# Sliding-window attention and a gated MLP on one Trainium2 core: all loads issued by GpSimd and cast to f16 on the way

## The chip, the cores and the metric

The kernel runs on one core of one Trainium2 chip. A core has five engines with an instruction stream each: TensorE (PE, matmuls into PSUM), VectorE (DVE), ScalarE (ACT), GpSimd (POOL) and SyncE (SP). Sixteen DMA engines move data between HBM and the on-chip memory SBUF; a DMA is issued from an engine's queue. The metric is the device time of one launch in microseconds (us), as the median of several runs.

## The reference

Eight batches, eight heads, 576 positions, head size 64, everything in float32. Attention over a causal window of 64 positions, then a gated MLP that mixes along the sequence:

```python
scores = (q @ k.T) / sqrt(64)                      # per batch and head
mask   = (rel >= 0) & (rel < 64)                   # rel = query position - key position
attn   = softmax(where(mask, scores, -1e9))
x      = (attn @ v) as [batch, 576, 8 * 64]
h      = relu(x @ w_in)                            # 512 -> 1024
u, v   = h[..., :512], h[..., 512:]
v_n    = (v - mean(v)) / sqrt(var(v) + 1e-6)       # over the 512 features
v_s    = w_spatial @ v_n + b_spatial               # along the sequence, 576 x 576
out    = (u * v_s) @ w_out                         # 512 -> 512
```

## The kernel before, in words

The work is cut into named steps, and a list in the source, `ORDER`, gives for every step its engine and its buffer or PSUM bank. `as_listed` takes the steps in the order of that list, so the list alone sets the order in which each engine meets its work; every engine runs its own steps strictly in that order and waits where a result or a buffer is not there yet. The planner's costs that stand at each step (such as `("DQ", 0.45)`) are not read when the kernel is built.

A step's name tells what it is. `b` is the batch (0 to 7), `g` the half of the heads (0, 1), `u` a pair of heads' sets within the half, `j` and `i` blocks of 128 positions or features.

- `ldk`, `ldq`, `ldv`: loads of k, q and v; `ldwin`, `ldwsp`, `ldb`, `ldwo`: loads of the weights. All are issued by SP (written DQ in the list), in float32, into staging tiles (`nat`, eight buffers, and `natv`, four).
- `ck`, `cq`, `cv`, `cwin`, `cwsp`, `cb`, `cwo`: casts from the staging tile to f16, on DVE, ACT or POOL, as the list says. They all go through the helper `cp` (L292 for ACT, L295, L298 and L300 for the others; the POOL forms are cut into pieces).
- `tk`, `tq`: transposes of k and q on DVE, in blocks of 32 x 32 pairs (L419). `sl`, `su`, `s4`: copies of v that shift it by 64 rows, from `hv` into `hs`.
- `S`: scores on PE (L479); `E`: exp on ACT (L486); `M`: the mask, a minimum with a constant tile on DVE (L489); `Z`: column sums (L502); `N`, `n`: the inverse of the sums, as exp(-ln) on ACT; `P`: the product with v (L514); `X`: the scaling, on DVE (L522). `_r` marks the last 64 positions, done apart.
- `V`: the half of the first MLP matmul that is normalised; `Vr` (relu, ACT), `Vb`, `Va` (mean and variance, DVE), `L1`, `L2` (ACT), `A` (the normalisation, DVE, L728). `U`, `Ur`: the other half. `W`, `We`: transposes of w_spatial. `G`: the spatial matmul; `Ge`: the gate on DVE (L797, L800). `O`: the output matmul; `Oe`: its copy out of PSUM; `st`: the store, issued by SP and at the end by ACT as well. `V4` of a batch carries the last block of `O` of the batch before.
- `D0` to `D26`: matmuls on a tile of zeros (L862), which keep PE busy while it waits at the start.

PE steps marked `PH` are issued as two matmuls of 64 columns of weights each (`halves`, L617), the others as one (L614). The constants come first, outside the list: the mask tile is built from `keep` by seven DVE instructions (L252 to L258), the identity and two rows of ones by POOL. The buffers matter as well: `hqk` (q and k in f16) has four, `hv` and `hs` (v and its shifted copy) four each.

Of the kernel before, what the change touches and what calls it, by code (L numbers as in the profile page):

```python
# [18 lines left out]
D24:PE:0 ldb:DQ:0 D5:PE:1 D21:PE:2 ldk0_0:DQ:1 ck0_0:DVE:0 tk0_0:DVE:0 D18:PE:3 D2:PE:2 D14:PE:2  # L19
D19:PE:3 D10:PE:0 ldq0_0:DQ:2 ldk0_1:DQ:3 ldv0_00:DQ:0 ldq0_1:DQ:4 ldv0_10:DQ:1 D3:PE:3 ldv0_11:DQ  # L20
cv0_10:POOL:0 ldk1_0:DQ:5 ck0_1:ACT:1 ldv0_12:DQ ldv0_13:DQ ldv0_01:DQ cq0_0:DVE:2 ldq1_0:DQ:6
tq0_0:DVE:1 ldv0_02:DQ D1:PE:2 S0_0:PE:0:1 tk0_1:DVE:2 D22:PE:0 E0_01:ACT:0 E0_00:ACT:1 cq0_1:DVE:3
tq0_1:DVE:3 D15:PE:3 D6:PE:1 D0:PE:2 D26:PE:0 D23:PE:3 S0_r:PE:1:0 E0_r0:ACT:0 E0_r1:ACT cv0_11:POOL
sl0_10:DVE:0 M0_00:DVE ldv0_03:DQ su0_10:DVE M0_01:DVE ck1_0:DVE:0 M0_r:DVE D8:PE:1 Z0_00:PE:2
ldv0_04:DQ ldwin110:DQ:7 ldv0_14:DQ ldwin111:DQ ldwin100:DQ:1 S0_1:PE:1:0 N0_00:ACT:0 E0_11:ACT:2
D16:PE:0 D7:PE:3 E0_10:ACT:3 M0_11:DVE Z0_01:PE:1 Z0_r:PE:2 D4:PE:0 Z0_11:PE:3 N0_r:ACT:1
N0_01:ACT:2 cv0_00:ACT:1 N0_11:ACT:3 ldwin101:DQ su0_11:DVE M0_10:DVE D12:PE:0 Z0_10:PE:2 D20:PE:1
sl0_11:POOL tk1_0:DVE:4 sl0_00:ACT:1 N0_10:ACT:4 n0_11:ACT n0_10:ACT cq1_0:POOL:2 tq1_0:DVE:5
ldq1_1:DQ:2 ldk1_1:DQ:3 P0_10:PE:0 P0_11:PE:3 cwin110:ACT n0_01:ACT D11:PE:1 cv0_01:POOL
ldwin000:DQ:4 ldwin010:DQ:5 ldwin001:DQ ldwin011:DQ ldwsp1:DQ:6 X0_10:DVE:0 su0_00:DVE X0_11:DVE  # L30
n0_00:ACT sl0_01:POOL cb:POOL su0_01:POOL S1_0:PE:0:1 D25:PE:2 D13:PE:1 P0_00:PE:0 X0_00:DVE:1
E1_01:ACT:3 s40_1:ACT P0_01:PE:2 D9:PE:3 cwin111:POOL cwin100:POOL cwin101:POOL ck1_1:POOL:1
s40_0:ACT E1_00:ACT:2 cwin010:POOL X0_01:DVE cwin001:POOL cwin011:POOL V0_2:PE:1 M1_01:DVE
Vr0_2:ACT:0 n0_r:ACT P0_r:PE:3 Z1_01:PE:0 V0_0:PE:2 ldwsp3:DQ:0 M1_00:DVE N1_01:ACT:5 Vr0_0:ACT:1
cq1_1:DVE:3 Z1_00:PE:1 V0_3:PH:0 V0_1:PE:2 N1_00:ACT:4 cwin000:ACT Vr0_3:ACT:2 Vr0_1:ACT:3
ldwsp0:DQ:7 ldwsp4:DQ:1 ldwsp2:DQ:2 cwsp1:POOL:6 ldv1_00:DQ:2 ldq2_0:DQ:3 X0_r:DVE:0 tq1_1:DVE:7
Vb0_2:DVE:0 V0_4:PE:3 tk1_1:DVE:8 S1_1:PE:1:0 cwsp3:POOL:0 cwsp0:POOL:1 Vb0_0:DVE:1 Vb0_3:DVE:2
Vr0_4:ACT:4 Va0_3:DVE Vb0_4:DVE:3 Va0_4:DVE Va0_0:DVE Va0_2:DVE Vb0_1:DVE:4 Va0_1:DVE U0_2:PH:1
U0_3:PH:0 ldk2_0:DQ:4 U0_4:PE:2 ldv1_01:DQ ldv1_02:DQ ldv1_03:DQ E1_11:ACT:1 E1_10:ACT:0 cwsp2:POOL
cq2_0:POOL:0 M1_10:DVE ldv1_10:DQ:3 Ur0_2:ACT:0 L10:ACT:0 ldv1_11:DQ ldv1_12:DQ ldv1_13:DQ L20:ACT  # L40
ldv1_14:DQ ldq2_1:DQ:5 ldv1_04:DQ ldk2_1:DQ:6 ldwo00:DQ:0 ldwo01:DQ Ur0_4:ACT:1 S1_r:PE:0:1
Z1_10:PE:3 U0_0:PE:1 ldwo10:DQ:7 ldwo11:DQ U0_1:PE:2 E1_r0:ACT:0 Ur0_3:ACT:2 E1_r1:ACT Ur0_0:ACT:3
N1_10:ACT:3 A0_0:DVE:0 A0_3:DVE:1 cwsp4:DVE Ur0_1:ACT:4 W1:PE:0 W3:PE:1 W2:PE:3 W0:PE:2 A0_1:DVE:2
A0_4:DVE M1_11:DVE We1:DVE M1_r:DVE n1_00:ACT We2:ACT We3:ACT A0_2:DVE:3 We0:DVE W4:PE:0 ldq3_0:DQ:1
ldk3_0:DQ:2 ldv2_00:DQ:1 ck2_0:POOL:2 We4:DVE D17:PE:3 Z1_11:PE:1 Z1_r:PE:2 G0_0:PH:3 G0_1:PH:0
tq2_0:DVE:2 n1_10:ACT N1_11:ACT:0 tk2_0:DVE:3 Ge0_0:DVE:0 cv1_00:ACT:2 n1_01:ACT sl1_00:POOL:2
n1_11:ACT su1_00:ACT N1_r:ACT:2 cv1_01:POOL Ge0_1:DVE:1 su1_01:DVE G0_3:PH:1 sl1_01:POOL
cv1_10:ACT:3 Ge0_3:DVE:2 cv1_11:DVE S2_0:PE:0:1 P1_01:PE:2 P1_00:PE:3 X1_00:DVE:2 G0_2:PH:0
sl1_10:POOL:3 ldv2_01:DQ ldv2_02:DQ su1_10:ACT sl1_11:ACT E2_01:ACT:3 n1_r:ACT su1_11:POOL
s41_1:POOL P1_10:PE:1 X1_01:DVE P1_11:PE:3 G0_4:PE:2 X1_10:DVE:3 X1_11:DVE U1_1:PH:1 cq2_1:POOL:3  # L50
E2_00:ACT:2 M2_01:DVE Ur1_1:ACT:5 Ge0_4:DVE:3 ck2_1:POOL:1 ldv2_03:DQ V1_2:PH:3 cwo01:POOL
cwo10:POOL cwo11:POOL Ge0_2:DVE:4 M2_00:DVE Z2_01:PE:2 s41_0:ACT Vr1_2:ACT:5 N2_01:ACT:1 U1_2:PH:1
Ur1_2:ACT:3 P1_r:PE:0 V1_1:PH:3 Vr1_1:ACT:6 cq3_0:POOL:0 Z2_00:PE:2 V1_3:PE:1 tq2_1:DVE:4
# [147 lines left out]
def kernel(  # L201
# [100 lines left out]
    def cost(n, a=True, d=True, p=True, d1=False):  # L302
# [613 lines left out]
```

## Time and profile before

| | us |
|---|---|
| median of 3 runs | 195.66 (195.64 to 197.04) |
| span of the profiled execution, from the first to the last instruction | 193.6 |
| PE busy | 184.9 |
| DVE busy | 163.7 |
| ACT busy | 157.1 |
| POOL busy | 87.4 |

The page gives no time of its own for the profiled execution beside the span; the median of the runs lies 2.1 us above that span. The granted TensorE clock is 1.00 in every stretch of the profile. Busy time does not count instructions that issue DMAs. Lines such as L489 are lines of the kernel before.

### The profile page before, as it was taken

To read this page: it belongs to the slowest core of one execution; us is meant where nothing else is said; L and a number is where in the kernel's file an instruction comes from. 1 tells how busy PE (TensorE), PEld (TensorE's weight loads), DVE (VectorE), ACT (ScalarE), POOL (GpSimd) and SP (SyncE) were. 2 spreads that over 40 slices of the span, in tenths; PEclk is the share of its full clock that TensorE was granted. 3 is DMA by queue.
4 is the path that set the end of the run, shared out by engine and by line. 5 is a ranking of instruction groups with operands and counts; after the bars stand their busy time and mean duration, and the time that the engine had idled before them with its cause. 6 is when DMAs were issued, how large, how long until landed. Compare 5 with 4: busy or idle time off the path is not lost.

```text
span 193.6 us, 7606 instructions
## 1 busy us (share of the span) xinstructions
PE 184.9 (95%) x3218; PEld 107.0 (55%) x3218; DVE 163.7 (85%) x304; ACT 157.1 (81%) x282; POOL 87.4 (45%) x161
## 2 busy tenths in 40 slices
PE   7798998999999999999999999999999999999991
PEld 2352534556556664656665656565756565665560
DVE  4899899999999999998999999998996967468331
ACT  2269998998999999899979999999999875706430
POOL 4027775849932986701956577615641520000000
PEclk9999999999999999999999999999999999999999
DMA  5999999899989997619987999669958000600445
GB/s 177 373 316 290 391 355 333 168 275 373 242 205 332 261 335 179 149 38 289 367 230 184 310 310 282 196 177 218 306 125 266 22 3 0 224 30 0 135 166 191
DMA packets 50421, 42.73 MB, mean 221 GB/s; under 512 B 39377, under 2 KB 39761, under 8 KB 50386
## 3 DMA queue, kind: packets, MB, share of 16 engines
q1 hardware_dynamic: 50162, 42.04, 73.3%
q8 instruction: 25, 0.41, 0.9%
q10 hardware_dynamic: 224, 0.20, 0.3%
q14 instruction: 10, 0.08, 0.1%
HBM read 32.79 MB, written 9.44 MB: 218 GB/s over the span
## 4 chain that ended last, share of the span: by engine, by line
PE 70%; DVE 13%; ACT 9%; DMA 3%; issue 2%; SPq 1%
PE bank L617 50%; PE bank L614 4%; PE pair L479 4%; PE bank L514 3%; DMA nk<-in_k_dram 3%; PE bank L502 3%; ACT e L486 3%; DVE qT L419 2%; PE bank L702 2%; DVE e L489 2%; DVE kT L419 2%; DVE st L671 2%; DVE g L797 1%; DVE x L522 1%; ACT lz L529 1%
## 5 line engine op out<-in xcount | busy, mean ns | idle before, releaser
L617 PE MATMUL bank<-wspT,vn 128*64 128x512 f16 (+3 forms) x530 | 39.1, 296 | 0.0
L486 ACT ACTIVATE e<-pair 128x1024 f16<-128x1024 f32 x32 | 32.0, 1030 | 1.6 <-PE pair L479 1.4
L797 DVE TENSOR_TENSOR g<-bank,ru 128x512 f16<-128x512 f32 (+1 forms) x36 | 23.3, 654 | 9.4 <-PE bank L617 7.0
L647 ACT COPY ob<-bank 128x512 f32<-128x512 f32 (+1 forms) x38 | 21.9, 591 | 9.7 <-PE bank L617 8.4
L669 ACT ACTIVATE vs<-bank 128x512 f16<-128x512 f32 (+1 forms) x40 | 23.8, 602 | 7.1 <-PE bank L705 5.6
L617 PE MATMUL bank<-x,win 128*64 128x512 f16 (+2 forms) x304 | 29.1, 327 | 0.0
L617 PEld LDWEIGHTS <-vn 128*64 128x64 f16 (+1 forms) x530 | 20.8, 111 | 13.2 <-issue 0.2
L671 DVE BATCH_NORM_STATS2 st<-vs 128x6 f32<-128x512 f16 (+1 forms) x40 | 26.0, 670 | 2.3 <-ACT vs L669 2.2
L298 POOL COPY hs<-hv 64x512 f16<-64x512 f16 (+1 forms) x36 | 20.1, 585 | 16.3 <-ACT hv L292 8.4
L617 PE MATMUL bank<-win,x 128*64 128x512 f16 x216 | 27.0, 379 | 0.0
L617 PE MATMUL bank<-wout,g 128*64 128x512 f16 (+1 forms) x208 | 24.7, 371 | 0.0
L522 DVE TENSOR_TENSOR x<-bank,lz 128x512 f16<-128x512 f32 x32 | 21.2, 684 | 3.5 <-PE bank L514 2.2
L489 DVE TENSOR_TENSOR e<-e,mask 128x1024 f16<-128x1024 f16 x32 | 23.0, 725 | 0.5 <-ACT e L486 0.4
L763 ACT ACTIVATE ru<-bank 128x512 f32<-128x512 f32 (+1 forms) x38 | 21.6, 584 | 1.5 <-PE bank L617 0.8
L295 POOL CAST hk<-nk 128x384 f16<-128x384 f32 x36 | 19.4, 574 | 7.1 <-DMA nk<-in_k_dram 6.7
L529 ACT ACTIVATE lz<-bank 128x512 f32<-128x512 f32 x32 | 19.0, 599 | 1.9 <-PE bank L502 1.6
L298 POOL CAST hv<-nv 128x512 f16<-128x512 f32 x18 | 11.7, 661 | 18.8 <-DMA nv<-in_v_dram 18.7
L419 DVE STREAM_TRANSPOSE kT<-hk 128x576 f32<-128x576 f32 x16 | 19.9, 1241 | 0.2 <-ACT hk L292 0.2
L419 DVE STREAM_TRANSPOSE qT<-hq 128x576 f32<-128x576 f32 x16 | 19.8, 1237 | 0.2
L531 ACT ACTIVATE lz<-lz 128x512 f32<-128x512 f32 x32 | 19.6, 642 | 0.0
L295 POOL CAST hq<-nq 128x384 f16<-128x384 f32 x27 | 14.9, 588 | 10.3 <-DMA nq<-in_q_dram 7.8
L617 PEld LDWEIGHTS <-win 128*64 128x64 f16 x304 | 14.4, 110 | 9.2
(91 smaller groups left out, 298.9 us busy)
## 6 DMA issues: line engine op xcount, KB each, us to landing
nk<-in_k_dram SPq DMA_DIRECT2D x16, 576.0 KB, 6.6
nq<-in_q_dram SPq DMA_DIRECT2D x16, 576.0 KB, 6.1
nv<-in_v_dram SPq DMA_DIRECT2D x64, 128.0 KB, 5.9
out_dram<-ob SPq DMA_DIRECT2D x14, 512.0 KB, 5.8
wi<-in_moe_w_in_dram SPq DMA_DIRECT2D x8, 256.0 KB, 5.8
ws<-in_moe_w_spatial_dram SPq DMA_DIRECT2D x4, 288.0 KB, 7.6
nv<-in_v_dram SPq DMA_DIRECT2D x16, 64.0 KB, 4.5
wo<-in_moe_w_out_dram SPq DMA_DIRECT2D x4, 256.0 KB, 7.2
```

The lines of the kernel that those rows point to most:

```text
L295: nc.gpsimd.tensor_copy(o[:, n:n + 384], i[:, n:n + 384])
L298: nc.gpsimd.tensor_copy(o[:, lo:hi, :, :], i[:, lo:hi, :, :])
L419: d = add(f"t{name}{b}_{g}", ("DVE", 1.09), key, lambda e: nc.vector.transpose(qt.t[:, :].rearrange("p (i j) -> p j i", j=18), h.t[:, :].b ...
L486: ex = add(f"E{b}_{g}{u}", ("ACT", 0.91), key, lambda e, u=u: nc.scalar.activation(e2[u].t[:, :, :], sc[u].t[:, :, :], AF.Exp, bias=0.0, s ...
L489: mins.append(add(f"M{b}_{g}{u}", ("DVE", 0.65), key, lambda e, u=u: nc.vector.tensor_tensor(e2[u].t[:, :, :], e2[u].t[:, :, :], mask[:, : ...
L522: lambda e, u=u, ob=ob, lz=lz: nc.vector.tensor_tensor(x.t[:, u, :], ob.t[:, :], lz.t[:, :], ALU.mult),
L617: nc.tensor.matmul(o[c:c + 64, :], w[:, c:c + 64], x, start=start, stop=stop)
L647: lambda e: (nc.vector.tensor_copy if last else nc.scalar.copy)(view(), m.t[rows, 0:n]),
L669: rl = add(f"Vr{b}_{j}", ("ACT", 0.49), key, lambda e: nc.scalar.activation(vs.t[0:jn, :], m.t[0:jn, :], AF.Relu), deps=[pv], acq=[vs], us ...
L671: s1 = add(f"Vb{b}_{j}", ("DVE", 0.6), key + 0.02, lambda e: nc.vector.bn_stats(st6.t[0:jn, 0:6], vs.t[0:jn, :]), deps=[rl], acq=[st6], us ...
L763: lambda e, m=m, ru=ru, n=n: nc.scalar.activation(ru.t[:, 0:n], m.t[:, 0:n], AF.Relu), deps=[pu], acq=[ru], uses=[m])))
L797: nc.vector.tensor_tensor(g.t[:, 0:n], m.t[:, 0:n], ru.t[:, 0:n], ALU.mult)
```

## The change

No load is issued by SP any more. Each load is issued by POOL, from the float32 tensor in HBM into a f16 tile, so the DMA casts it on the way; v too goes straight into `hv`. The staging tiles and all casts of loads on chip are gone. The weights come in few DMAs (two for w_in, two for w_spatial, one for w_out), into merged tiles. `hqk` and `hv` have eight buffers instead of four. The mask and the constants become steps of the list: `keep` and `consts` on POOL, `mask` on DVE, and the mask minimum waits for `mask`. 38 warm-up steps stand in the place of 27 (13 of two matmuls, 25 of one, all over 512 columns), and the whole list is in a new order, with new engines for the shifted copies of v, and other PSUM banks.

The core of the diff (of the list only the first lines of the new one and its part around the end of the attention):

```diff
 ORDER = """
...
+D0:PE:0 D1:PE:1 D2:PE:2 D3:PE:3 D4:PE:0 D5:PE:1 D6:PE:2 D7:PE:3 D8:PE:0 D9:PE:1 D10:PE:2 D11:PE:3
+D12:PE:0 ldq0_0:POOL:0 ldk0_0:POOL:1 tk0_0:DVE:0 ldq0_1:POOL:2 tq0_0:DVE:1 S0_0:PE:0:1 tq0_1:DVE:2
+E0_00:ACT:0 E0_01:ACT:1 ldk0_1:POOL:3 tk0_1:DVE:3 keep:POOL mask:DVE M0_00:DVE M0_01:DVE D13:PE:1
...
+N6_11:ACT:1 n6_11:ACT E7_10:ACT:1 E7_11:ACT:0 sl7_00:POOL:3 su7_00:POOL ldv7_10:POOL:6 Va5_1:DVE
+X6_10:DVE:1 X6_11:DVE M7_00:DVE O4_0:PH:1 U5_1:PH:2 M7_10:DVE Va5_0:DVE O4_1:PH:3 Oe4_0:ACT:1
+Ur5_1:ACT:3 Vb5_2:DVE:3 V6_3:PH:0 Vr6_3:ACT:5 Va5_2:DVE M7_11:DVE S7_r:PE:0:1 Vb6_3:DVE:2
+Z7_11:PE:1 N7_11:ACT:4 s47_0:DVE Va5_4:DVE Z7_10:PE:2 N7_10:ACT:3 L15:ACT:1 L25:ACT Oe4_1:ACT
+A5_1:DVE:4 A5_4:DVE O4_2:PH:0 Oe4_2:ACT:0 V6_0:PH:1 sl7_10:POOL:2 ldv7_14:POOL Vr6_0:ACT:6
+s47_1:POOL s46_1:POOL U5_0:PH:2 Ur5_0:ACT:5 V6_1:PH:3 Z7_00:PE:0 O4_3:PH:1 N7_00:ACT:5 Oe4_3:ACT
...
-NWARM, NFILL, FILL = 27, 2, 9
-BUFS = {"nat": 8, "natv": 4, "hqk": 4, "qkT": 9, "hv": 4, "hs": 4, "e2": 4, "er": 1, "lz": 6,
+NWARM, NFILL, FILL = 38, 25, 1
+BUFS = {"hqk": 8, "qkT": 9, "hv": 8, "hs": 4, "e2": 4, "er": 1, "lz": 6,
...
+    kept = add("keep", ("POOL", 0.7), -2.0, emit_keep)
+    masked = add("mask", ("DVE", 2.0), -2.0, emit_mask, deps=[kept])
+    def emit_consts(e):
+        make_identity(nc, id16[:])
+        for i in range(NSB):
+            nc.gpsimd.memset(vn4_t[i][64:65, :], 1.0)
+    ids = add("consts", ("POOL", 1.8), -2.0, emit_consts)
...
+            ld = add(f"ldwin{half}", ("POOL", 0.85), key + 0.01 * (1 - half),
+                     lambda e, cs=cs: nc.gpsimd.dma_start(
+                         w_in_all[:, :, cs], moe_w_in[:, cs].rearrange("(r p) f -> p r f", r=4)))
...
+            add("ldwsp0", ("POOL", 0.85), key, lambda e: nc.gpsimd.dma_start(
+                wsp_nat[:, 0:4, :], moe_w_spatial[0:512, :].rearrange("(t p) s -> p t s", t=4))),
...
-            n = buf("nat", f"n{name}{b}_{g}")
-            ld = add(f"ld{name}{b}_{g}", ("DQ", 0.45), key, lambda e: nc.sync.dma_start(
-                n.t[:, :], src[b, 4 * g:4 * g + 4, :, :].rearrange("h (i j) d -> (h i) (j d)", j=18)),
-                acq=[n], nbytes=1.57, n=128)
             h = buf("hqk", f"h{name}{b}_{g}")
-            c = add(f"c{name}{b}_{g}", cost(1152), key,
-                    lambda e: cp(e, h.t[:, :], n.t[:, :]), deps=[ld], acq=[h], uses=[n])
+            ld = add(f"ld{name}{b}_{g}", ("POOL", 0.55), key, lambda e: nc.gpsimd.dma_start(
+                h.t[:, :], src[b, 4 * g:4 * g + 4, :, :].rearrange("h (i j) d -> (h i) (j d)", j=18)),
+                acq=[h])
...
+            ld = add(f"ldv{b}_{g}{n}", ("POOL", 0.5 + 0.36 * w), key + 0.002 + 0.0001 * n,
+                     lambda e, lo=lo, hi=hi: [nc.gpsimd.dma_start(
+                         hv.t[:, c, :, :],
+                         v[b, 4 * g:4 * g + 4, 128 * c:128 * c + 128, :].transpose([1, 0, 2]))
+                         for c in range(lo, hi)],
+                     deps=done[:1], acq=[hv] if n == 0 else [], uses=[hv] if n else [])
...
+        ld = add(f"ldv{b}_{g}4", ("POOL", 0.65), key + 0.0025, lambda e: nc.gpsimd.dma_start(
+            hv.t[0:64, 4, :, :], v[b, 4 * g:4 * g + 4, 512:576, :].transpose([1, 0, 2])),
+            deps=[done[0]], uses=[hv])
...
-                n = 512 if i < NWARM - NFILL else 128
+                n = 512
```

More of the change, by code (lines that the diff above doesn't have):

```diff
@@ L24 @@
[L24 to L53, printed above, removed]
@@ L120 @@
-E7_00:ACT:3 Oe4_4:ACT:0 X6_11:DVE Vr5_4:ACT:4 cq7_1:ACT:1 O4_0:PH:0 Oe4_0:ACT:0 M7_00:DVE Va5_0:DVE
-M7_01:DVE Vb5_4:DVE:1 U6_2:PH:2 O4_1:PH:1 V6_0:PH:3 O4_2:PH:0 Ur6_2:ACT:5 Oe4_1:ACT st4_0:DQ
-Vr6_0:ACT:2 cv7_00:POOL:2 Va5_2:DVE tk7_1:DVE:5 Va5_4:DVE tq7_1:DVE:6 L15:ACT:1 L25:ACT A5_0:DVE:4
-A5_2:DVE:5 Oe4_2:ACT:1 Z7_01:PE:2 Z7_00:PE:1 O4_3:PH:3 N7_01:ACT:1 N7_00:ACT:5 Oe4_3:ACT V6_1:PH:0
-S7_1:PE:1:0 V6_3:PH:2 sl7_00:POOL:2 A5_1:DVE:6 A5_4:DVE A5_3:DVE:7 G5_3:PH:1 Vr6_1:ACT:0 Vb6_1:DVE:0
-su7_00:POOL ldv7_13:DQ E7_11:ACT:0 E7_10:ACT:2 n7_00:ACT P7_00:PE:3 G5_4:PH:0 S7_r:PE:0:1
@@ L292, in cp @@
             nc.scalar.copy(o, i)
-        elif e == "POOL" and len(i.shape) == 2 and i.shape[1] > 1000:
-            for n in (0, 384, 768):
-                nc.gpsimd.tensor_copy(o[:, n:n + 384], i[:, n:n + 384])
         elif e == "POOL" and len(i.shape) == 4 and i.shape[1] > 2:
```

332 lines of the change are left out of this document (143 added, 189 removed).

## The prediction

> **What bounds the kernel now.** I read the page first: the shares, the slices, and the chain that ended last.
>
> ```profile
> PE 184.9 (95%) x3218; PEld 107.0 (55%) x3218; DVE 163.7 (85%) x304; ACT 157.1 (81%) x282; POOL 87.4 (45%) x161
> ...
> GB/s 177 373 316 290 391 355 333 168 275 373 242 205 332 261 335 179 149 38 289 367 230 184 310 310 282 196 177 218 306 125 266 22 3 0 224 30 0 135 166 191
> ...
> PE 70%; DVE 13%; ACT 9%; DMA 3%; issue 2%; SPq 1%
> ```
>
> TensorE (PE) is busy in 95% of the span and carries 70% of the chain, so only what shortens PE's own list, its start or its tail can help. The busy time is not all work. The warm-up matmuls have a group of their own, 16.1 us, in the grouped lines; then I cut the span into stretches (columns: length, then PE, PEld, DVE, ACT, POOL busy, granted clock, DMA share, GB/s).
>
> ```profile
> L862 PE MATMUL bank<-scratch 128*128 128x512 f16 (+1 forms) x68 | 16.1, 380 | 1.3 <-DVE scratch L237 1.3
> ```
>
> ```profile
> 5.26:38.69 33.43, 30.46 (x493) 14.98 (x492) 31.66 (x52) 26.90 (x48) 19.46 (x29) 1.00 1.05 317
> 38.69:60.00 21.31, 21.26 (x432) 12.00 (x428) 20.51 (x37) 20.02 (x38) 12.80 (x23) 1.00 0.93 284
> 60.00:100.00 40.00, 39.67 (x706) 24.82 (x697) 38.64 (x71) 37.82 (x70) 23.57 (x44) 1.00 0.84 242
> 100.00:140.00 40.00, 40.00 (x884) 24.60 (x874) 37.45 (x64) 38.44 (x67) 22.79 (x43) 1.00 0.87 240
> 140.00:152.07 12.07, 12.07 (x248) 7.17 (x246) 10.29 (x22) 11.95 (x21) 2.73 (x5) 1.00 0.63 175
> 152.07:189.45 37.38, 37.38 (x490) 21.94 (x486) 22.82 (x51) 20.31 (x40) 3.72 (x6) 1.00 0.23 78
> ```
>
> From 38.69 us on, PE is packed; ahead of it lies the filler. But VectorE (DVE) is nearly as full: 31.66 of 33.43 us in the first stretch, 97% from 60 to 100. So two engines are critical at once: DVE sets the start, PE the rest, and DVE follows it closely until the last attention steps.
>
> **The point at which I compare.** Z7_11, the column sums of the last batch's last pair of heads, is where DVE's heavy work ends. It starts at 152.07 us. Up to there DVE has been busy for 31.66+20.51+38.64+37.45+10.29 = 138.6 of 146.8 us since 5.26, so it was idle for 8.2. Behind it PE has 37.4 us left.
>
> ```profile
> 152.07 0.38 PE L502 MATMUL bank<-e,ones 128*64 128x512 f16 x2
> ...
> 177.04 3.62 PE L617 MATMUL bank<-wout,g 128*64 128x512 f16 x32
> 180.50 5.14 PE L617 MATMUL bank<-wspT,vn 128*64 128x512 f16 x80
> 185.46 3.20 PE L617 MATMUL bank<-wout,g 128*64 128x512 f16 x32
> ...
> 190.31 0.54 ACTq L838 DMA_DIRECT2D out_dram<-ob  x1
> ```
>
> The last row is the last store, issued second on ACT's queue; from the end of PE (189.45) to the end of the span (193.6) it is 4.15 us. Starts of neighbours give PE's prices: four O steps in 180.50-177.04 = 3.46, so 0.865 each, or 0.216 for 512 columns (V and U are as long); five G steps in 185.46-180.50 = 4.96.
>
> **The new list, PE.** Counting the two lists: behind Z7_11 the new one has all the steps that the old one has there, and 13 more: O4_2, O4_3, U5_0, U6_2, V6_0, V6_1 (6 x 0.865 = 5.2), G5_2 to G5_4 (3.0) and four short Z and P steps (each passes 512 columns through both halves of the array side by side: 0.22, so 0.9). So PE has 37.4+9.1 = 46.5 us left. The work is the same; attention has moved 9 us earlier against the rest. DVE must therefore be done with it about 9 us earlier, and 8.2 us of idle time is what it had.
>
> **The new list, DVE, up to that point.** Rows for what is removed, added and moved:
>
> ```profile
> L300 DVE CAST hq<-nq 128x1152 f16<-128x1152 f32 x4 | 3.3, 826 | 0.0
> L300 DVE CAST hk<-nk 128x1152 f16<-128x1152 f32 x2 | 1.9, 965 | 1.7 <-DMA nk<-in_k_dram 1.7
> L300 DVE COPY hs<-hv 64x512 f16<-64x512 f16 x4 | 1.2, 294 | 0.1
> L300 DVE COPY hs<-hv 64x768 f16<-64x768 f16 x1 | 0.7, 655 | 0.0
> L300 DVE COPY hs<-hv 64x1024 f16<-64x1024 f16 x1 | 0.4, 422 | 0.0
> L300 DVE COPY hs<-hv 64x256 f16<-64x256 f16 x1 | 0.2, 222 | 0.0
> ...
> L728 DVE TENSOR_SCALAR vn<-vs,mv,ln 128x512 f16<-128x512 f16 x32 | 12.1, 422 | 2.2 <-ACT ln L718 1.9
> L522 DVE TENSOR_TENSOR x<-bank,lz 128x512 f16<-128x512 f32 x32 | 21.2, 684 | 3.5 <-PE bank L514 2.2
> ```
>
> ```profile
> 0.81 0.15 POOL L244 MEMSET keep<- 128x64 f16 x1 [0.29 <-POOLq L902]
> 1.21 0.38 SPq L412 DMA_DIRECT2D nk<-in_k_dram  x1
> 1.61 0.18 DVE L252 COPY mask<-keep 128x64 f16<-128x64 f16 x1 [0.32 <-POOL keep L247]
> 3.27 0.29 DVE L258 COPY mask<-mask 128x512 f16<-128x512 f16 x1
> 5.26 0.76 DVE L300 CAST hk<-nk 128x1152 f16<-128x1152 f32 x1 [1.66 <-DMA nk<-in_k_dram]
> 8.20 1.15 ACT L292 CAST hk<-nk 128x1152 f16<-128x1152 f32 x1 [6.11 <-DMA nk<-in_k_dram]
> 38.69 3.42 PE L617 MATMUL bank<-wspT,vn 128*64 128x512 f16 x30
> ```
>
> Removed: six q/k casts, 5.2 us, and three smaller casts, about 1.4 at the price of the 64x1024 copy and above; 6.2 in all after an overlap of 0.06 each with the neighbour (my estimate: the groups add up to some 16 us more than the 163.7 busy, over 304 instructions). Moved: the seven mask steps ran from 1.61 to 3.56 while DVE waited for its first load; in the new list they stand after four transposes, on the path: +1.95. Copies into hs: eight before; 25 now, of which 15 are small (0.22 to 0.29), one kind is 64x1024 (0.42, 3) and one 64x768 (6, between 0.35, the larger copy's price scaled, and the 0.655 of its single row); with the overlap +3.5 to +5.3. I take +3.5, because the larger copy needed only 0.42. The order leaves for later five A steps (0.42), one X and, at its price, one Vb and one Ge (0.68 each) and small ones: -4.2. Sum: 138.6-6.2+1.95+3.5-4.2 = 133.7.
>
> **Contention.** The mask minimum (M) is one form throughout, and yet:
>
> ```profile
> L489 DVE TENSOR_TENSOR e<-e,mask x32: 649/682/1062, 12.8 to 151.8; 128x1024 f16<-128x1024 f16 x32
> ...
> 45.79 1.86 POOL L295 CAST hk<-nk 128x384 f16<-128x384 f32 x3
> 45.90 0.94 DVE L489 TENSOR_TENSOR e<-e,mask 128x1024 f16<-128x1024 f16 x1
> ```
>
> Beside a GpSimd (POOL) cast it takes 0.94 instead of 0.65. With the casts gone, M can win between 0 and 32 x (0.72-0.65) = 2.2 us (0.72 is the 23.0 us of its group over 32); below zero if issuing loads disturbs it as much or more. I take 1.5, as most POOL work that reads SBUF goes: 132.2. [...]
>
> **The first load.** Issued at 1.21, landed at 5.26: 4.05 us. The third load landed at 8.20, so each further one takes (8.20-5.26)/2 = 1.47. POOL can issue at 0.81; k0_0 comes second, so 0.81+4.05+1.47 = 6.3 at SP's price. No row shows a load issued by POOL; the price lies between 1 us less (smaller writes) and 3 us more (the longest issue in the row below). I take +0.9: DVE's first transpose at 7.2 instead of its first work at 5.26. [...]
>
> ```profile
> L433 SPq DMA_DIRECT2D nv<-in_v_dram x80: 367/681/3307, 2.6 to 147.7; - x80
> ```
>
> **The start.** Up to G0 (38.69) DVE loses five of the six casts (4.4) and defers M1_r and one weight copy (1.0), gains the mask (1.95) and some copies (0.9) and begins 1.9 later: -0.7. PE has U0_3 (0.87) still to do at that point: even. M now waits for the mask, the mask for `keep`, and `keep` stands behind four loads on POOL; all of DVE's list queues behind it, but four issues end near 3.5 us and the mask is due near 12, so this wait costs nothing. The identity (`consts`) stands behind seventeen loads, at some 17 us, and is due with the transposes of w_spatial near 30. Fewer warm-up matmuls (51 for 68) lie in PE's waiting time, at no gain.
>
> Loads that must land before U0: 9.33 MB (batch 0, q and k of batch 1, w_in, w_spatial). At the 343 GB/s that slices 2 to 7 of the GB/s line average, the last lands at 4.9+0.9+8.74/0.343 = 31.3, where 0.59 MB is the first load. The new list puts 3.7 us of PE steps from U0_4 up to G0, so 33.5 is early enough: covered, with 2 us to spare.
>
> **POOL.** 118 DMAs at the 0.5 to 0.7 us that SP needs for one is 59 to 83 us, 18 copies some 18 more, in place of 87.4 busy: POOL has room. Its copies wait in line ahead of later loads, but the list issues loads up to a batch ahead (eight buffers for q/k and for V). Stores alone stay with SP, at no cost or gain: PE does not wait for them. The merged weight tiles and the longer list of halved steps change no price above.
>
> **Sum.** 7.2 + 132.2 + idle. For DVE's idle I take 3% (4.0 us), near the 3.4% of 60 to 100, its fullest long stretch: Z7_11 at 143.4. PE's own path has its filler unchanged: 152.07-9.1 = 143.0. Both meet. 143.4+46.5, and 3.8 at the end (the last DMA no longer stands behind another on ACT's queue), give a span of 193.7 against 193.6. The median of the runs, 195.66, lies 2.1 above that span; so I predict 195.8: no change.
>
> **Rivals.** Two more views bear on them: the chain in order of time, at the start, and the DMA lines of the page.
>
> ```profile
> 17.62 0.50 ACT hv L292
> ...
> 20.71 0.51 ACT win L292
> ...
> 23.20 0.71 ACT hs L292 x2
> ...
> 25.60 1.06 DVE hq L300
> ```
>
> ```profile
> q1 hardware_dynamic: 50162, 42.04, 73.3%
> ...
> HBM read 32.79 MB, written 9.44 MB: 218 GB/s over the span
> ```
>
> 1. *The start gets shorter* (faster). Casts of ACT (0.50+0.51+0.71 = 1.7) stand on the chain beside DVE's, and my sum counts DVE alone. With these gone and the first load 1.2 earlier, PE's path comes to 143.0-2.9 = 140.1, and DVE's, with 2 us of idle time and all 2.2 of M, to 6.0+131.5+2.0 = 139.5. Then 140.1+46.5+3.8+2.1 = 192.5. For: the rows above. Against: the mask and the copies take ACT's place on DVE. 0.30.
> 2. *The loads come later* (slower). The start is DMA-bound (share 1.05 in the first stretch). At 20% less rate w_in's second half lands at 5.8+8.74/0.274 = 37.7, 4.2 after the 33.5, and all PE work behind U0 moves by that: 200.0. It decides from about 8% less. For: V keeps its short rows, half as long in f16. Against: half the bytes to write. 0.14.
> 3. *DVE becomes the bound* (slower): it keeps its 8.2 us of idle time, because its fixed order waits for PE and ACT as now; 4.2 more than in the sum: 200.0. 0.10.
> 4. *Issues and DVE block each other* (slower): 118 issues last as long as the casts did, so M stays at 0.72 and DVE's copies wait as well: +1.5 to +4, about 198.5. [...] Against: the long kinds of DVE work (M, X, transposes) have run beside POOL with a loss only where POOL reads, as far as the rows show. 0.07.
> 5. *The cast on the way halves the rate*, so that the change does not do what it says: loads are 32.8 of 42.0 MB, 57 of the 73.3%; doubled, with the rest, 130% of the span: 250 us. 0.03.
>
> The likeliest case has 0.36 and reaches from 193.9 to 197.4. A measurement tells 1% from no change. Faster by over 1% (under 193.7): rival 1 but for a little, and the low end of the main case, 0.32. Slower (over 197.6): rivals 2 to 5, 0.32. Within: 0.36. Below 190.5 and above 200.8 I leave out about one in ten each.
>
> **What would show it.** Right: first transpose near 7.2, G0 near 38, Z7_11 near 143, DVE over 96% busy between. M near 0.66 shows the contention gone; M or A longer than now, rival 4. U0 waiting for win, rival 2. Z7_11 well before 142 with PE packed means rival 1. Wrong altogether: q/k loads that land over 3 us apart.

## The result and the profile after

The changed kernel took 203.54 us (median of four runs, 202.36 to 206.54) against 196.2 for the kernel before on the same chip: 1.035 times as long, with a 95% interval of 1.028 to 1.042. The forecast was 195.8 us, with a range of 190.5 to 200.8. The change made the kernel slower, and by more than any rival that I had named would have made it, but the one of a halved load rate. In seven groups of runs one execution is longer than the others, by up to 7% (214.36 us with four output tiles, where the other three took 198.69 to 200.61); the medians here count it, the ratios leave it out. The profiled run took 204.24 us, its span is 202.5.

The page of the changed kernel: the busy times, TensorE's granted clock in the 40 slices, the chain by engine, and the loads of V in POOL's list.

```profile
PE 187.8 (93%) x3276; PEld 111.0 (55%) x3276; DVE 160.1 (79%) x310; ACT 148.2 (73%) x269; POOL 98.7 (49%) x160
...
PEclk9999999999999999699999999999999999999998
...
PE 62%; DVE 14%; ACT 10%; DMA 7%; issue 4%; SPq 0%; DVEq 0%; ACTq 0%
...
L385 POOL DMA_DIRECT2D hv<-in_v_dram x64 | 48.0, 769 | 9.2 <-issue 3.4
```

PE was busy for 95% of the span and is now busy for 93%; DVE went from 85 to 79%, ACT from 81 to 73%. So these three wait more than before, and none of them is a tighter bound. (POOL's 49% can't be set beside its 45%: its busy time now holds its issues of loads, of which the V row above alone has 48.0 us, while SP's issues before were not counted.) The chain says what they wait for: 7% DMA, which is all stores (no store stood on the chain before), and 4% "issue" instead of 2%, time in which an engine waited for nothing that the profile shows; its two longest pieces, 1.95 and 1.73 us, are PE's. The forecast compared the kernels at Z7_11, which starts at 152.00 here. Below are the stretches from DVE's first transpose to the first G step, from there to Z7_11, and from there to the end of PE (columns: length, then PE, PEld, DVE, ACT, POOL busy, granted clock, DMA share, GB/s):

```profile
6.93:35.53 28.60, 26.61 (x470) 15.51 (x468) 27.55 (x55) 22.78 (x41) 20.99 (x34) 1.00 1.42 177
35.53:152.00 116.47, 108.97 (x2244) 67.81 (x2244) 104.99 (x190) 96.73 (x174) 70.34 (x110) 0.99 1.02 136
152.00:198.55 46.55, 46.53 (x552) 25.54 (x552) 26.65 (x60) 27.40 (x55) 1.72 (x4) 1.00 0.25 86
```

The first G step came at 35.53, 3.2 us earlier than before (38.69): the start did get shorter. But in the middle stretch PE stands idle for 116.47-108.97 = 7.5 us, where the kernel before, in its own (38.69 to 152.07), was idle for 0.4. The next rows show what ends PE's longer waits, and ACT's wait that stands behind one kind of them (columns: sum, times, longest):

```profile
PE pair L423 <- issue: 2.6, 2, 1.9
PE bank L561 <- ACT ob L591: 2.1, 3, 1.5
PE bank L458 <- issue: 1.7, 1, 1.7
```

```profile
ACT ob L591 <- DMA out_dram<-ob: 5.8, 4, 2.7
```

That makes 2.1 us behind ACT's copies into the output tiles (`ob`, two of them), which wait for stores that have not left their tile, and 2.6+1.7 = 4.3 us without a releaser ("issue"), of which 1.95 and 1.73 are single waits. After the wait of 1.95 us (78.88 to 80.83) PE's granted clock was 0.50 for 3.4 us (81.19 to 84.60), so a stretch of ten us has a clock of 0.83:

```profile
80.00:90.00 10.00, 9.18 (x160) 5.36 (x161) 6.18 (x12) 7.20 (x13) 6.48 (x11) 0.83 1.08 118
```

3.4 us at half clock cost 1.7. So 7.5 + 1.7 = 9.2 us went in the middle; without them the span would be 193.3, near the 193.7 of the sum. Only 2.1 of them stand directly behind late stores. The experiments had to find out why the stores are late and what the waits without a releaser are.

### The profile page after: what moved, and what is told of

Same layout as the page of the kernel before. It is cut to its first block, busy times and chain, and to the rows that moved or that the text cites. A ratio compares the mean times of both kernels' runs of the same rounds, so it can differ in the third digit from the quotient of the medians.

```text
span 202.5 us, 7546 instructions
## 1 busy us (share of the span) xinstructions
PE 187.8 (93%) x3276; PEld 111.0 (55%) x3276; DVE 160.1 (79%) x310; ACT 148.2 (73%) x269; POOL 98.7 (49%) x160
## 4 chain that ended last, share of the span: by engine, by line
PE 62%; DVE 14%; ACT 10%; DMA 7%; issue 4%; SPq 0%; DVEq 0%; ACTq 0%
PE bank L561 38%; PE bank L558 8%; DMA out_dram<-ob 7%; PE bank L806 5%; DVE st L615 3%; DVE e L433 3%; PE pair L423 2%; ACT e L430 2%; DVE g L741 2%; PE bank L458 2%; PE bank L646 2%; DVE x L466 2%; PE bank L446 2%; ACT ob L591 2%; ACT lz L473 2%
## 5 line engine op out<-in xcount | busy, mean ns | idle before, releaser
L385 POOL DMA_DIRECT2D hv<-in_v_dram x64 | 48.0, 769 | 9.2 <-issue 3.4
L430 ACT ACTIVATE e<-pair 128x1024 f16<-128x1024 f32 x32 | 31.9, 1024 | 12.5 <-PE pair L423 12.4
L561 PE MATMUL bank<-wspT,vn 128*64 128x64 f16 (+3 forms) x560 | 35.1, 274 | 0.4 <-DVE g L741 0.2
L561 PE MATMUL bank<-x,win 128*64 128x512 f16 (+2 forms) x368 | 31.3, 308 | 1.6 <-ACT ob L591 1.5
L272 POOL COPY hs<-hv 64x512 f16<-64x512 f16 (+1 forms) x26 | 15.3, 619 | 34.7 <-PE bank L541 19.1
L561 PE MATMUL bank<-win,x 128*64 128x512 f16 x256 | 32.1, 380 | 0.0
L561 PE MATMUL bank<-wout,g 128*64 128x512 f16 (+1 forms) x224 | 28.1, 382 | 0.5 <-ACT ob L591 0.5
L433 DVE TENSOR_TENSOR e<-e,mask 128x1024 f16<-128x1024 f16 x32 | 21.8, 698 | 1.6 <-ACT e L430 1.4
L561 PEld LDWEIGHTS <-win 128*64 128x64 f16 x368 | 16.2, 111 | 12.3 <-issue 2.7
L561 PEld LDWEIGHTS <-x 128*64 128x64 f16 x256 | 15.9, 110 | 9.8
L672 DVE TENSOR_SCALAR vn<-vs,mv,ln 128x512 f16<-128x512 f16 (+1 forms) x40 | 15.6, 438 | 4.7 <-ACT ln L662 4.6
```

The costliest lines, as they stand in the source:

```text
L385: lambda e, lo=lo, hi=hi: [nc.gpsimd.dma_start(hv.t[:, c, :, :], v[b, 4 * g:4 * g + 4, 128 * c:128 * c + 128, :].transpose([1, 0, 2])) for ...
L430: ex = add(f"E{b}_{g}{u}", ("ACT", 0.91), key, lambda e, u=u: nc.scalar.activation(e2[u].t[:, :, :], sc[u].t[:, :, :], AF.Exp, bias=0.0, s ...
L433: mins.append(add(f"M{b}_{g}{u}", ("DVE", 0.65), key, lambda e, u=u: nc.vector.tensor_tensor(e2[u].t[:, :, :], e2[u].t[:, :, :], mask[:, : ...
L561: nc.tensor.matmul(o[c:c + 64, :], w[:, c:c + 64], x, start=start, stop=stop)
```

## The experiments

The theories, numbered as in the expectations: (1) V's short rows hold the DMA engines longer when they are cast on the way; (2) the new list as such makes the waits; (3) POOL's issuing is too slow; (4) stores come late to ACT, either (4a) because of the loads' traffic or (4b) because of their place in SP's list; (5) PE waits for its own code. All times are medians; the kernel before, measured beside each of them, had 195.79 to 196.2. The figure behind a time is its ratio to the kernel before, with the 95% interval.

### What a row costs: loads alone

The kernel holds only loads, in six groups one after the other.

> Loads alone, in six groups one after the other, the result left at zero: eight V loads of 128 KB by SP in f32, the same eight by POOL in f32, the same cast to f16 by POOL, eight by POOL with long rows cast to f16, four q loads by SP in f32, four k loads by POOL cast to f16. By (1) the short rows take 18 ns in the first two groups and 32 in the third, and the q/k pieces 8% more with the cast than without. If it is POOL's queue and not the cast that costs, the second group is as slow as the third.

The packets in the trace, by the bytes that they write (my own grouping of the packet records; medians and the sum over all of a kind divided by 16 engines):

```
loads alone     SP, f32, V rows       256 B x4096   18 ns    4.6 us
                POOL, f32, V rows    4096 B x256   182 ns    3.7 us
                POOL, cast, V rows    128 B x4096   32 ns    8.2 us
                POOL, cast, long V    512 B x1024   60 ns    4.5 us
                SP, f32, q           4608 B x512   178 ns    6.2 us
                POOL, cast, k        2304 B x512   192 ns    6.6 us
kernel before   SP, f32, V rows       256 B x36864  18 ns   44.7 us
changed kernel  POOL, cast, V rows    128 B x36864  32 ns   74.1 us
```

So (1) has its premise: under the cast a row of V holds an engine 1.8 times as long, one of q or k only 8% longer. It is the cast and not POOL's queue: uncast, POOL's rows go out 16 to a packet, at 11 ns a row. Over the whole kernel it is 29 us more of all 16 engines. Whether that costs time is another question.

### V's loads, undone and changed

In the changed kernel, V again in f32 by SP, with staging, and cast by POOL just ahead of its first use:

```diff
-ldv2_00:POOL:4 ... sl2_00:DVE:0
+ldv2_00:DQ:0 ... cv2_00:POOL:0 sl2_00:DVE:0
```

> The changed kernel, but V is loaded in f32 by SP into staging tiles and cast to f16 by POOL just ahead of its first use; q, k and the weights are still cast on the way. Three theories. (1) V's rows: in the changed kernel each of V's 36,864 short rows holds a DMA engine for 32 ns (18 ns before the change), 29 us more of all 16 engines, and loads, stores and the fetches of PE's code queue behind that. (2) The new list: its order of steps makes the waits, whoever loads. (3) POOL's issuing: 0.76 us for each of V's loads, one after the other and behind POOL's copies, brings the loads too late. By (1) the rows are back at 18 ns and the time is 193 to 197. By (2) it stays at 200 to 204. By (3) POOL has 80 issues fewer, so also 193 to 198: this run tells (2) from the others.

204.72 us, 1.047 (1.044 to 1.051). V's rows are at 18 ns again and nothing is gained, which is nearest to what (2) expected. But the run is no clean test, as its waits of POOL show:

```profile
POOL hv L291 <- DMA nv<-in_v_dram: 79.3, 17, 14.1
```

POOL stands for 79 us in front of casts whose data has not landed, and the q and k loads of its list stand behind them. A second version casts V of batches 0 and 1 on the way, so that the start is that of the changed kernel, and has four output tiles:

> The changed kernel with four output tiles, and V from batch 2 on loaded in f32 by SP into four staging tiles and cast by POOL (V of batches 0 and 1 cast on the way as in the changed kernel, so that the start is the same). V's rows at 18 ns again for three quarters of V, 64 issues fewer on POOL, 12 batches of casts more. By (1) and (3): 195 to 198. If V's loads on SP now hold up the stores behind them, or the casts on POOL the q/k loads behind them, 199 to 204.

203.54 us, 1.037 (1.032 to 1.042), for the same reason: POOL's casts wait 50.1 us for V's data, and SP's V loads now stand behind stores that wait for ACT. Both runs took away the short rows and put a new queue in their place; they say nothing for or against (1). The next one leaves the queues alone and changes only the rows:

```diff
-v[b, 4 * g:4 * g + 4, 128 * c:128 * c + 128, :].transpose([1, 0, 2]))
+v[b, 4 * g + c, 0:512, :].rearrange("(p r) d -> p r d", r=4))
```

> The changed kernel, but the four main loads of V of each half batch take one head each, with four neighbouring rows of V on one partition: the same bytes and the same number of loads, still cast on the way, in 512-byte pieces instead of 128-byte ones. The rows of V so stand on other partitions than attention needs, so that part of the result is another. By (1) V's time on the DMA engines falls from 74 us to under 45, the waits for stores and loads go, and the time is 192 to 197. By (2) it stays at 200 to 204. By (3) it stays there as well if an issue on POOL still takes 0.76 us, and falls in proportion if an issue gets shorter.

202.96 us, 1.034 (1.027 to 1.041), where the changed kernel has 1.035. V's time on the engines fell from 74 to 41 us, and the time by half a microsecond, which the noise covers. V's short rows alone are not the cause.

### One part alone, in the old list

In the kernel before, V loaded by POOL and cast on the way, or loaded by POOL in f32 with the casts kept, or q and k alone loaded by POOL and cast on the way:

```diff
-ldv0_00:DQ:0 ... cv0_00:ACT:1
+ldv0_00:POOL:0 ...                 (V cast on the way)
+ldv0_00:POOL:0 ... cv0_00:ACT:1    (V in f32 by POOL)
-ldk0_0:DQ:1 ck0_0:DVE:0
+ldk0_0:POOL:0                      (q and k cast on the way)
```

> The kernel before, with its list, but V is loaded by POOL and cast on the way (V's casts and staging are gone, hv has eight buffers); q, k and the weights as before, by SP. By (1) V's rows take 32 ns and the DMA engines have some 29 us more to do: slower than before, 198 to 204. By (2) the old list keeps its time: 194 to 197. By (3) slower as well, 198 to 204, since 80 issues join POOL's casts.

> The kernel before, with its list, but V is loaded by POOL in f32, not cast on the way; V's casts stay where they were. By (1) V's rows stay near 18 ns and the time within 1.5% of before: 194 to 198.5. By (3) the same 80 issues on POOL cost as much as in the kernel with V cast on the way, or more, since POOL also keeps V's casts: 198 to 206. By (2) 194 to 197.

> The kernel before, with its list, but q and k are loaded by POOL and cast on the way (their casts are gone, six f32 tiles stay for the weights, eight tiles for the cast q and k); V and the weights as before. 32 issues of 0.55 us join POOL's list, 63 casts of 0.58 us leave it. (1) and (4), (5): the q/k loads hold the DMA engines only some 8% longer, V stays at 18 ns, so 193 to 197. (3), POOL's issuing: a q/k load now stands behind POOL's casts and copies; with 32 loads that are up to a few us later each, 198 to 206.

The times: 215.75 us (1.102, 1.096 to 1.108) with V cast, 225.36 (1.151, 1.145 to 1.157) with V in f32, 199.63 (1.017, 1.012 to 1.022) with q and k cast. The two with V are far beyond what any theory had expected. The uncast loads, whose rows took 11 ns in the loads alone, cost most (POOL keeps V's casts there), so once more it isn't the cast on the way alone. The loads in POOL's list, a copy of DVE, and a stretch of the chain of waits, in the kernel with V cast:

```profile
3.13 6.67 POOL L449 DMA_DIRECT2D hv<-in_v_dram  x8
```

```profile
21.49 0.22 DVE L316 COPY hs<-hv 64x256 f16<-64x256 f16 x1 [8.87 <-DMA hv<-in_v_dram]
```

```profile
4.74 16.73 DMA hv<-in_v_dram
```

POOL has issued eight loads by 9.80, but the chain follows one V load for 16.73 us, to 21.47. DVE's copy of V waits for it, the next mask step stands behind that copy in DVE's list, and PE, which needs the mask step, waits 8.93 us (to 22.49). So V comes late at the start there. Whether POOL's issuing (3) or the many loads in flight make it late, these runs don't separate. The new list puts q and k first and spreads V's issues, so this says nothing of the changed kernel.

### Taking the load off, and taking the late stores off

In the changed kernel, four output tiles instead of two; then no loads of V from batch 2 on; then both; then four output tiles with V's long rows:

```diff
-        "x": 4, ... "g": 10, "ob": 2, "ob4": 1, "ln": 2}
+        "x": 4, ... "g": 10, "ob": 4, "ob4": 1, "ln": 2}
```

```diff
-        hv = buf("hv", f"hv{b}_{g}")
+        hv = buf("hv", f"hv{b}_{g}") if b < 2 else HV[1, g]
```

> The changed kernel with four tiles for the output in place of two; nothing else. In its profile ACT waits 5.8 us for stores that have not left their tile, and PE waits behind ACT for 2.1 us; PE also waits 4.4 us for its own code ("issue"), after one of these waits it runs at half clock for 3.4 us. (4) Late stores: a store takes 6 to 8 us beside the loads, and the list takes the tile again sooner than that; with four tiles ACT's wait for stores is gone and the time falls by 2 to 4 us, to 199 to 201.5. (5) Late code: only PE's fetches count, and the time stays within 1 us. (2), the list itself: PE waits at the same places for something else, and the time stays within 1 us.

> The changed kernel without the loads of V from batch 2 on: these batches use V of batch 1, so the result is another; all copies and all other steps stay. The traffic of the loads falls by 14 MB in f32, POOL has 60 issues fewer. If what is lost is lost to the DMA traffic ((4) and (5) together), PE's waits for code and for the output tiles go, the clock stays at 1.00, and the time is 193 to 197. If it is the order of the list, PE waits as much as now and the time is 200 to 203.

> The changed kernel with four output tiles and without the loads of V from batch 2 on (these batches use V of batch 1, so the result is another). Four output tiles alone gave 200.0, the missing loads alone 197.9. If late stores (4) and the traffic of V's loads account for the whole loss, together they give 194 to 196.5, with PE waiting under 1 us behind 36 us. If something in the list itself is left, 197 to 198, as without the loads alone.

> The changed kernel with four output tiles, and V in long rows (512-byte pieces; rows on other partitions, so the result is another). V's time on the DMA engines falls from 74 to about 41 us at the same bytes and the same number of loads. If the rest of the loss (200.0 against 195.7) comes from V's short rows under the cast (1), 195.5 to 198. If it comes from the bytes and the moment of the loads, whatever their rows, 199 to 201.

```
changed kernel                       203.54   ratio to before 1.035 (1.028 to 1.042)
four output tiles                    200.0                    1.019 (1.013 to 1.024)
no V loads from batch 2 on           197.89                   1.008 (1.006 to 1.011)
both                                 197.76                   1.008 (1.005 to 1.011)
four output tiles, long V rows       198.87                   1.016 (1.010 to 1.021)
```

Four tiles give back 3.5 us, as (4) had it, the missing loads 5.7 (a little short of the 193 to 197 that the traffic as the whole cause would have given), and both together no more than the loads alone: the two touch the same waits. So late stores and V's traffic both have a part in the loss. V's short rows are worth at most about 1 us (200.0 to 198.87, with intervals that overlap) once the stores are out of the way; that lies between the two forecasts. 1.6 us stay with both off, which is neither V's loads from batch 2 on nor the number of output tiles; I had expected 194 to 196.5 there.

### Why the stores are late

With two tiles a copy needs the tile's last store to have landed; these are ACT's 5.8 us. SP's own list in the changed kernel, from 50 to 110 us (L600 is the small store of a batch, L606 the two large ones; a row of several runs from the first start to the last end):

```profile
55.42 16.31 SPq L600 DMA_DIRECT2D out_dram<-ob  x2
71.77 1.47 SPq L606 DMA_DIRECT2D out_dram<-ob  x2
97.54 0.47 SPq L600 DMA_DIRECT2D out_dram<-ob  x1
98.06 1.15 SPq L606 DMA_DIRECT2D out_dram<-ob  x2
```

In this stretch each pair of large stores follows, within a microsecond, a small store. ACT's last copy of batch 0 ended at 59.97, its two stores went out at 71.77 and 72.41. In the list they stand behind `st1_4`, the small store of the *next* batch, and SP takes its list in order; `st1_4` waits for ACT's copy at 71.24. Batch 1 repeats it behind `st2_4`: its tiles were full at 85.26 and 91.53, the stores issued at 98.06 and 98.69, and the chain of waits shows the price:

```profile
97.54 0.47 SPq L600
98.01 0.04 issue
98.06 6.25 DMA out_dram<-ob
...
104.41 0.59 ACT ob L591
105.00 0.04 issue
105.04 1.05 PE bank L561 x8
```

SP issues, the store lands 6.25 us later, only then may ACT copy into the tile, and only then has PE a bank. The chain meets the same links once more with batch 2, whose store stands behind the small store of batch 3:

```profile
127.73 0.47 SPq L600
...
128.25 8.12 DMA out_dram<-ob
...
136.40 0.59 ACT ob L591
...
137.03 2.77 PE bank L561 x44
```

There PE's wait is the 1.5 us that the table of waits has as the longest behind ACT. In the kernel before, the two stores of batch 0 stand ahead of the small store of batch 1 (L656) and went out at 63.7 and 66.5:

```profile
63.68 1.05 SPq L662 DMA_DIRECT2D out_dram<-ob  x1
...
66.51 0.50 SPq L662 DMA_DIRECT2D out_dram<-ob  x1
...
77.81 0.56 SPq L656 DMA_DIRECT2D out_dram<-ob  x1
```

So the changed kernel was run with nothing moved but the large stores of batches 0 to 6, each right behind the copy that fills its tile:

```diff
-Oe0_3:ACT ... st1_4:DQ ... st0_1:DQ ... st0_0:DQ
+Oe0_1:ACT st0_0:DQ ... Oe0_3:ACT st0_1:DQ ... st1_4:DQ
```

> The changed kernel, with two output tiles as it has; only SP's list is another: each 512 KB store of batches 0 to 6 stands right behind the second copy that fills its tile. In the changed kernel the two stores of batch 0 are issued 12 us after their last copy, those of batch 1 6 and 12 us after it, because in SP's list they stand behind the small store of the next batch, which waits for ACT. (4b) That order is what makes the tiles come late: then two tiles do, ACT's 5.8 us of waiting for stores go, and the time is that of four tiles, 199 to 200.5. (4a) The stores are late because of the traffic of the loads, wherever they stand: then the time stays over 202.

198.07 us, 1.010 (1.005 to 1.015), with two tiles and all of V's casts and short rows: 5.5 us back by the medians (4.9 by the ratios). That is a little better than expected, and about what leaving V's loads out gave. SP's list, the stretches as above, and what is left of PE's larger waits:

```profile
57.19 2.85 SPq L605 DMA_DIRECT2D out_dram<-ob  x2
60.09 12.11 SPq L599 DMA_DIRECT2D out_dram<-ob  x2
82.02 6.56 SPq L605 DMA_DIRECT2D out_dram<-ob  x2
```

```profile
35.40:144.91 109.51, 106.60 (x2243) 66.24 (x2242) 103.87 (x190) 96.01 (x173) 71.58 (x111) 1.00 1.08 144
144.91:191.60 46.69, 46.60 (x563) 25.62 (x552) 26.83 (x60) 27.47 (x55) 1.34 (x3) 1.00 0.24 86
```

```profile
PE pair L422 <- issue: 1.4, 1, 1.4
...
PE bank L560 <- ACT ob L590: 0.3, 1, 0.3
```

Now the large stores of batch 0 leave at 57.2 and 59.7, the wait behind ACT's copies is 0.3 instead of 2.1, the clock is 1.00 throughout, and Z7_11 comes at 144.91 instead of 152.00. (4b) holds, and (4a) as I had put it, late wherever they stand, falls: a large store takes about as long from issue to landing as in the changed kernel (3.6 us in the median, 4.0 there), and from its early place it lands in time. The traffic has its part all the same, since without V's loads the late place costs little (197.89). The mirror image puts the stores of batches 0 and 1 of the kernel before where the changed kernel has them:

```diff
-st0_4:DQ st0_1:DQ ... st0_0:DQ ... Oe1_4:ACT:0
+st0_4:DQ ... Oe1_4:ACT:0 st1_4:DQ st0_0:DQ st0_1:DQ
```

> The mirror image: the kernel before, with only the stores of batches 0 and 1 moved in SP's list behind the small store of the next batch, as the changed kernel has them. In the kernel before, the two stores of batch 0 are issued at 63.7 and 66.5 us and have landed by 76.5, just as ACT takes the first of the tiles again (76.7); behind the small store of batch 1, whose copy ends at 75.5, they would land near 82 to 85. Those of batch 1 would be issued at 91 instead of 87 and 90. (4b), the place in SP's list: ACT waits some 5 us for the tiles of batch 0, of which PE's other work hides a part: 197 to 201. If stores may stand anywhere in the old list, 195 to 196.5.

204.69 us, 1.042 (1.033 to 1.051): moving six stores in SP's list (the two large ones of batches 0 and 1, and the small ones of 1 and 2) costs the old kernel 8.9 us by the medians, 8.2 by the ratio. That is more than I had expected and about as much as the whole change cost. Its waits of PE and of ACT, and its chain from the small store on:

```profile
PE bank L614 <- ACT ob L647: 5.3, 2, 4.2
```

```profile
ACT ob L647 <- DMA out_dram<-ob: 7.6, 2, 5.6
```

```profile
76.71 0.51 SPq L656
77.22 0.04 issue
77.27 0.59 SPq L662
77.86 0.04 issue
77.90 5.70 DMA out_dram<-ob
83.60 0.02 issue
83.62 0.59 ACT ob L647
84.22 0.04 issue
84.26 2.72 PE bank L614 x20
```

It is the same chain, link by link, in a kernel without a single cast on the way. One PE wait of 4.2 us came of it, and PE was slower behind it: the next four O matmuls took 1.66 us (84.26 to 85.92), the 16 of 64 columns behind them 0.99, the scores 0.85, where the same take 0.865, 0.56 and 0.60 elsewhere. That is 1.5 us more, together 5.7; the mean clock of this run is 0.986. SP issues the loads too in this kernel, and three V loads now stand behind the store that waits; what they add isn't separated.

### The waits without a releaser

These are PE's "issue" waits. They stand at fixed places. The counts of matmuls (PE) and weight loads (PEld) up to three of them in the changed kernel, and up to one in a kernel with the stores moved and all halved steps done whole:

```profile
0.00:65.90 65.90, 62.00 (x1118) 36.86 (x1119) 57.69 (x111) 51.83 (x93) 50.38 (x84) 1.00 1.29 158
0.00:78.87 78.87, 74.25 (x1374) 44.31 (x1374) 69.14 (x134) 61.88 (x112) 60.49 (x99) 1.00 1.26 158
0.00:106.30 106.30, 99.14 (x1886) 59.47 (x1886) 91.75 (x172) 83.03 (x150) 78.12 (x127) 0.98 1.26 161
```

```profile
0.00:67.00 67.00, 63.78 (x990) 31.57 (x991) 57.14 (x112) 51.99 (x93) 48.06 (x79) 1.00 1.29 168
```

1118, 1374 and 1886 differ by 256 and 512; 990, in a list with quite other matmuls, is 128 less than 1118. 128 matmuls with their weight loads are 256 instructions. The page has 25 packets on a queue that it calls instruction ("q8 instruction: 25, 0.41" MB, so 16 KB each) beside 3276 matmuls and as many weight loads, 6,552 in all: 262 instructions of PE for each packet, close to the 256. So by the counts PE waits where a packet ends. The times of these packets agree (my reading of the packet records, on the span's clock):

```
                        packet lands    PE goes on    behind it by
changed kernel            79.36            80.83          1.5
changed kernel           106.58           108.04          1.5
stores moved              65.62            67.08          1.5
stores moved, whole       67.39            68.70          1.3
```

So I take them as waits for code. That the loads or stores delay this code is not shown. The wait behind the 1886th matmul stands in four other kernels too, at 1.15 to 1.39 us: with four tiles, without V's loads, with both, and with four tiles and long rows. For the kernel with both:

```profile
0.00:101.38 101.38, 97.11 (x1886) 58.77 (x1886) 91.10 (x172) 83.64 (x152) 48.20 (x83) 1.00 0.93 148
```

```profile
PE bank L470 <- issue: 1.1, 1, 1.1
```

The packet in front of this wait took 0.95 us (100.34 to 101.29), and the median of the 25 in the changed kernel is 0.96, but its fetch began only when PE was at its 1868th matmul, 18 ahead of the wait. With the stores moved, where this wait is gone, the packet's fetch began at the 1786th (100.53), and PE went through. So this wait needs neither V's traffic nor late stores, and it is 1.15 of the 1.6 us that were left with both off. Why the fetch starts early or late is open. The kernel meant to test (5) halves the code of most steps:

```diff
-V0_1:PH:0 ... U0_0:PH:1 ... G0_1:PH:3
+V0_1:PE:0 ... U0_0:PE:1 ... G0_1:PE:3
```

> The same with all matmuls that the list splits into two halves of 64 columns done whole (128 columns): the same columns pass, with about half of PE's instructions in these steps. (5) PE's waits without a releaser end exactly every 256 matmuls (after the 1118th, 1374th and 1886th; with its weight load each, 512 instructions), so they are waits for PE's code, which comes in pieces over the same DMA engines: with far fewer instructions these waits go, and the time falls by 1.5 to 3 us more, to 196.5 to 198.5. If these waits have another cause, or if whole matmuls cost as much elsewhere, it stays within 1 us of the kernel with the stores moved.

204.14 us, 1.039 (1.036 to 1.042): 6 us slower than with halves, where I had expected it to be faster or the same. The instruction queue moved 20 packets instead of 25 and one wait of 1.58 us stayed, at such a boundary; but PE was busy for 193.2 us instead of 185.2, so the price of whole matmuls hides whatever the smaller code was worth. The places and the packets speak for (5); a run that removes the waits and nothing else wasn't made.

## Why the prediction was wrong

**The step that failed** is one sentence of the part on POOL: "Stores alone stay with SP, at no cost or gain: PE does not wait for them." I had looked at the stores' engine and number, which stay, and not at their order in SP's list, which the change turns over. With it fell the line of the sum that DVE would be idle for 4.0 us, and that PE's own path, "its filler unchanged", would run through. What the trace shows in its place is 12.5 us of idle time for DVE up to Z7_11 (152.00-6.93-27.55-104.99) and 9.2 us lost by PE. With nothing but the stores moved, Z7_11 comes 7.1 us earlier, and PE's idle time in the middle falls from 7.5 to 2.9 us, with no half clock behind it.

The 4.0 us were too small even so: with the stores moved DVE is still idle for 6.9 us (144.91-6.90-27.29-103.87). I had taken the share of idle time from the old list, and nothing on record said that the new list would keep it.

**The rest of the sum held in its totals:**

- The first transpose was forecast at 7.2 and came at 6.93. The range of the unknown price (a load issued by POOL) was wider than it had to be.
- DVE's work from there to Z7_11: forecast 132.2, measured 27.55+104.99 = 132.5. That this fits is in part luck. The copies into hs take 8.3 us up to Z7_11 (25 copies) instead of 2.8 (8), so 5.5 more where the sum has 3.5. Against that, the mask steps of the last 64 positions, which the sum left as they were, fell from 4.6 to 3.0 us.
- PE's work behind Z7_11: forecast 46.5, measured 46.55. From PE's end to the span's: forecast 3.8, measured 202.5-198.55 = 3.95.
- G0 was forecast at 38 and came at 35.53: rival 1's start was real. It is no gain by itself, since the list has put more of PE's work behind it; with the stores moved, PE is idle for 2.9 us from there to Z7_11, and Z7_11 still starts at 144.91 (forecast 143.4).
- M lost 1.2 us of its 23.0; the forecast was 1.5. The median stays at 681 ns (682 before). What fell is the number of long ones: five of 32 took over 0.87 us before, each beside a cast or copy of POOL, and two do now, both beside POOL's copies into hs. Beside issues alone none took over 0.70 us.

```profile
L433 DVE TENSOR_TENSOR e<-e,mask x32: 649/681/1047, 13.2 to 154.7; 128x1024 f16<-128x1024 f16 x32
```

With each large store right behind its copy the same change takes 198.07 us, 1.2% above the forecast and inside the range. So for the loads, the casts and DVE's list the forecast came near, in part by the luck named above. It was wrong for the order of the list, which I had checked for PE, DVE and POOL but not for SP.

**The rivals.** Rival 2 (the loads come later) named a place that was not hit: PE did not wait for w_in. Rival 3 (DVE keeps its 8.2 us of idle time) had a part of the truth: DVE is idle for 12.5 us, of which 6.9 stay when the stores are moved, so more than my 4.0; but most of the loss came from the stores and not from there. Rival 4 (issues and DVE block each other) needed M to stay as long as before; beside issues alone none took over 0.70. Rival 5 (the cast halves the rate) was right in part of its premise, since V's rows take 1.8 times as long, and wrong in its price: 33 us of V's engine time taken away were worth 0.6 us, as long as the queues stood as they do. An issue on POOL cost 0.77 us for a V load, over the 0.5 to 0.7 I had assumed; POOL had room for that. None of the rivals was a wait of ACT for a store, although in the trace of the kernel before a large store takes up to 10.0 us from issue to landing, and only its early place hides that.

**What stays open.** Moving the stores alone takes most of the loss away, and moving them back makes it anew in the old kernel; that much is shown. The way from the stores to the time is shown only in part: of PE's waits, 2.1 us stood directly behind ACT's copies (0.3 with the stores moved), and the waits without a releaser fell at the same time from 4.3 to 1.4 us, and with them went the half clock. Why late stores should bring those waits isn't known. And 198.07 against 196.18 beside it leaves 1.9 us, of which the one wait of 1.42 us, which I take for one for code, may be most. No version that was run beats the kernel before.

## What to carry to other kernels

When a change brings a new order, follow every queue in it, the stores' own too: for each buffer that is used again, read off when its last reader is issued and what stands ahead of it on that queue. Here a large store whose tile was full at 59.97 left at 71.77, behind one that waited; ACT, with two tiles to fill, waited 5.8 us for such stores, and PE 2.1 us behind ACT. What the DMAs cost on the DMA engines said little of the time: 33 us less with long rows were worth 0.6 us. Whether a wait ended on one said more: six stores moved in SP's list cost the old kernel 8.9 us.

## What the hardware showed that was not expected

- Behind a wait of PE of 1.95 us in the changed kernel the granted clock was 0.50 for 3.4 us. The kernel with all of V loaded by SP, where the longest wait shown is 2.4 us, ran at a mean clock of 0.972; the old list with V cast, with a wait of 8.9 us, at 0.967. The length alone doesn't decide: behind a wait of 1.73 us in the changed kernel the clock stayed at 1.00 (106.00 to 120.00), and the kernel with q and k cast, with a wait of 3.2 us, had a mean of 0.998.
- The instruction queue moved 25 packets of 16 KB beside 6,552 instructions of PE in the changed kernel, and 20 beside 5,144 with the split matmuls done whole: 262 and 257 for each. At places that the counts and packet times put at the end of one, PE stood still for up to 1.95 us.
- Halves were nevertheless cheaper here: with 704 pairs of halves made whole (2572 matmuls instead of 3276) PE was busy 8.0 us longer (193.2 against 185.2), 11 ns for each pair.
- A row of 256 bytes of f32 took 18 ns by SP, 11 ns by POOL uncast (16 rows to a packet) and 32 ns by POOL cast to f16. In pieces of 512 bytes written, the cast took 60 ns, half as much per byte.
